# Second PSUM pair, row transfers on SyncE and a new product order in an attention, expert and swish kernel

## The chip, the cores and the metric

The kernel runs on one core of a Trainium2 chip. The metric is device time in microseconds: the median of three runs of the kernel before is 1480.46 us (1477.26 to 1486.97). One execution was profiled: 1479.06 us, its span 1477.0 us, with a mean granted TensorE clock of 0.939 of full speed. All durations below are of that execution.

## The reference

Three layers follow each other, on 4608 tokens of 512 numbers:

```python
scores = scale * (q_c @ k_c.T); attn = softmax(scores); x = attn @ v_c   # chunks of 64
expert_idx = argmax(normalised x @ normalised expert_emb.T / tau)        # one of 8 experts
h = max(x[mask] @ w1[e], 0); x[mask] = gate_w * (h @ w2[e])              # 512 -> 1024 -> 512
h = x @ w_in; g = h * sigmoid(1.702 * h); out = g @ w_out                # 512 -> 2048 -> 512
```

## The kernel before

**Attention** (to about 235 us) makes the tokens x, stores them in DRAM (`xs`) as two 16-bit halves, and sorts them by expert: two tables `mtab` in DRAM hold, at the sorted place of a token, its scale and its number (the sum of the two tables is the entry).

**The expert stage** (about 235 to 750 us) goes over 39 tiles of 128 sorted tokens. For tile i:
- `find(i)` reads the 128 entries of both tables (tile `mt`), by an indirect DMA that POOL issues;
- `fetch(i)` adds the two (POOL) and gathers the tokens (`xg`, an indirect DMA of POOL);
- `turn(i)` transposes them by a DMA of SyncE into `xTm`, of which there are two;
- `mm1(i)` is the first layer: 96 products of 128x128 in two PSUM banks `ph`; ACT (line 895) writes the high half of `hT`, DVE (line 896) the low half;
- `mm2(i)` is the second layer in a bank `py`; `mm2_evac(i)` scales the result on ACT and DVE into the row tile `y` and stores it to `ys` by an indirect DMA of POOL (line 955).

The loop issues, for tile i: `mm1(i)`, `turn(i+2)`, `fetch(i+3)`, `find(i+4)`, `swap(i+1, 1)`, `mm2(i-1)`, `swap(i, 2)`, `mm2_evac(i-1)`, and one step `dec`. `swap` splits the next expert's weights (ACT line 786, DVE line 791) and loads the ones after, under an `If` that is taken only where a tile begins a new expert. The first matmul of `mm1` waits for the bank, the third for the low half of the split of w1, or, where no split is made, for DVE's branch past it (line 840); the splits and the branches stand behind `hT` in DVE's program.

One step of `dec` reads a block of the swish weights (64-bit numbers), rebuilds 32-bit ones on DVE (lines 1222, 1223, 1226, 1229), and makes sums and halves of the previous block: ACT takes the high half (line 1119), POOL subtracts it for the low half (line 1120) and makes differences (line 1128). There are 32 blocks, 16 of `w_in` and 16 of `w_out`; a block of `w_out` sees four such pieces.

**The swish stage** (about 750 to 1477 us) goes over 9 groups j of 512 tokens. `up(j, s)`, four times, makes the hidden values; `down(j)` multiplies by `w_out` with seven products in place of eight, each of 48 matmuls, operands `G[o]`. The hidden values of the four quarters s are `zq[s, ...]`; `mix1` to `mix4` make the sums that four of the products need (`put(o, s, z)`: ACT high half, POOL low half into `G[o]`). `later` is a list of such steps, `mixes(n)` issues n of them, and `more` issues the sums of the next group. A product accumulates on a bank: X takes products 0, 4 and 5, V takes 3 and 6. Between two products on one bank, `keep` copies the sum so far to SBUF on ACT (`t1`, `t2`, `t5`). The weights of the products come by a ring of three loads of 1 MB on SyncE's queue.

Each engine runs its own program in the order in which it is written, and every DMA of SyncE waits for the DMA eight before it on that queue.

Of the kernel before, what the change touches and what calls it, by code (L numbers as in the profile page):

```python
# [9 lines left out]
F32 = mybir.dt.float32  # L10
# [7 lines left out]
ENG = mybir.EngineType  # L18
# [16 lines left out]
def kernel(  # L35
# [13 lines left out]
    nc = tc.nc  # L49
    B, H, S, D = q.shape  # L50
    NT, DM = out.shape
    NE = emb.shape[0]
# [10 lines left out]
    SURE = 39  # L63
    NPART = 24
    NSURE = 3
# [8 lines left out]
    ps = ctx.enter_context(tc.tile_pool(name="ps", bufs=1, space=PSUM))  # L74
# [6 lines left out]
    mtab = [dr.tile([NE * NT, 2], F32, name=f"mtab{a}") for a in range(2)]  # L81
    YP = 2 * DM + 8
    ys = dr.tile([NT + 128, YP], F16, name="ys")
# [59 lines left out]
    for t in vt:  # L143
# [15 lines left out]
        out=tri16, in_=ones16, pattern=[[1, 128]], compare_op=ALU.is_gt, fill=0.0,  # L159
# [19 lines left out]
    for m_, op_ in ((lt_m, ALU.is_lt), (le_m, ALU.is_le)):  # L179
        nc.vector.tensor_tensor(  # L180
            out=m_, in0=io_e.unsqueeze(1).to_broadcast([128, NE, NE]),
# [9 lines left out]
    for t in mtab:  # L191
        nc.sync.dma_start(
            out=t.rearrange("(p a r) c -> p a (r c)", p=128, a=4),
            in_=ztab.to_broadcast([128, 4, NE * NT * 2 // 512]),
# [396 lines left out]
    idx_g = const.tile([128, MAXT], I32, name="idx_g")  # L591
    idx_y = const.tile([128, MAXT], I32, name="idx_y")
# [168 lines left out]
    def reg(ap, engines, hi):  # L761
        return nc.values_load(ap, engines=engines, min_val=0, max_val=hi)
# [83 lines left out]
    mt_t, xg_t, xTm_t, hT_t = {}, {}, {}, {}  # L846

    def find(i):
        mt_t[i] = [mo.tile([128, 2], F32, tag=f"mt{a}", name=f"mt{a}", bufs=6) for a in range(2)]
        for a in range(2):  # L850
            nc.gpsimd.indirect_dma_start(  # L851
                out=mt_t[i][a][:, :], out_offset=None, in_=mtab[a][:, :],
                in_offset=bass.IndirectOffsetOnAxis(ap=idx_g[:, i:i + 1], axis=0),
            )
# [20 lines left out]
    ph_t = {}  # L875

    def mm1_part(i, q):

        xT = xTm_t[i]
        if q == 0:  # L880
            ph_t[i] = [ps.tile([128, 4, 128], F32, tag="A", name="ph", bufs=2) for _ in range(2)]
            hT_t[i] = mo.tile([128, 2 * KF, 128], F16, tag="hT", name="hT", bufs=2)
        p, hT = ph_t[i][q // 2], hT_t[i]
        for f in (2 * q, 2 * q + 1):
            fs = slice(f * 128, (f + 1) * 128)
            for c in range(KD):
                for wt, a in ((w1H, c), (w1H, KD + c), (w1L, c)):
                    nc.tensor.matmul(  # L888
                        p[:, f % 4], wt[:, c, fs], xT[:, a, :],
                        start=(c == 0 and a == 0 and wt is w1H), stop=(c == KD - 1 and wt is w1L),  # L890
                    )
        if q % 2 == 0:
            return
        hi, lo = (hT[:, o + q // 2 * 4:o + q // 2 * 4 + 4] for o in (0, KF))
        nc.scalar.activation(out=hi, in_=p, func=AF.Relu)  # L895
        nc.vector.scalar_tensor_tensor(out=lo, in0=p, scalar=0.0, in1=hi, op0=ALU.max, op1=ALU.subtract)  # L896
        if q == 3:
            xTm_t.pop(i)
            ph_t.pop(i)
# [23 lines left out]
    def mm2_evac(i):  # L923
        hT_t.pop(i)
        p = py_t.pop(i)
        mt = mt_t.pop(i)
        y = mo.tile([128, YP], F16, tag="y", name="y", bufs=2)
        ysq = mo.tile([128, DM], F16, tag="ysq", name="ysq", bufs=1)
        s = mo.tile([128, 4], F32, tag="ys", name="ysc", bufs=2)
        si = s.bitcast(I32)  # L930
        c_i = mt.bitcast(I32)[:, 0:1]
        tail = y[:, 2 * DM:YP].bitcast(I32).rearrange("p (a two) -> p a two", two=2)
        n = (YP - 2 * DM) // 4
        nc.scalar.activation(out=ysq, in_=p, func=AF.Square, scale=2.0 ** -20, accum_out=s[:, 0:1])  # L934
        nc.vector.tensor_scalar(si[:, 3:4], c_i, EXP_BITS, None, op0=ALU.bitwise_and)
        nc.vector.tensor_copy(tail[:, :, 0], mt.bitcast(I32)[:, 1:2].to_broadcast([128, n]))
        nc.vector.tensor_scalar(s[:, 0:1], s[:, 0:1], Y_MIN * 2.0 ** -40, None, op0=ALU.max)
        nc.vector.tensor_scalar(
            si[:, 1:2], si[:, 0:1], 24, 23, op0=ALU.logical_shift_right, op1=ALU.logical_shift_left
        )  # L940
        nc.vector.tensor_scalar(
            si[:, 1:2], si[:, 1:2], -1.0, float((BIAS + Y_TOP - 20) << 23), op0=ALU.mult, op1=ALU.add
        )
        nc.vector.scalar_tensor_tensor(  # L944
            out=si[:, 2:3], in0=c_i, scalar=MAN_BITS, in1=si[:, 1:2], op0=ALU.bitwise_and, op1=ALU.bitwise_or
        )
        nc.scalar.activation(out=y[:, 0:DM], in_=p, func=AF.Copy, scale=s[:, 2:3])  # L947
        nc.vector.scalar_tensor_tensor(
            out=y[:, DM:2 * DM], in0=p, scalar=s[:, 2:3], in1=y[:, 0:DM], op0=ALU.mult, op1=ALU.subtract
        )  # L950
        nc.vector.scalar_tensor_tensor(
            out=tail[:, :, 1], in0=si[:, 3:4].to_broadcast([128, n]), scalar=float(BIAS << 23),
            in1=si[:, 1:2].to_broadcast([128, n]), op0=ALU.add, op1=ALU.subtract,
        )
        nc.gpsimd.indirect_dma_start(  # L955
            out=ys[:, :], out_offset=bass.IndirectOffsetOnAxis(ap=idx_y[:, i:i + 1], axis=0),
            in_=y[:, :], in_offset=None,
        )


    def v_due(n):
# [288 lines left out]
    dec = big_split()  # L1250
    yT_t, id_t, R_t = {}, {}, {}
    NRING = 3
    PROD = ((B11, 0), (B21, 1), (T4, 2), (T1, 3), (T2, 4), (T3, 5), (B22, 6))
    LASTD = NSURE + 33
    for i in range(NSURE, SURE):
        mm1(i)
# [69 lines left out]
    banks = [ps.tile([128, 512], F32, tag="A", name="pa", bufs=2) for _ in range(2)]  # L1326
    banks.append(ps.tile([128, 512], F32, tag="C", name="pc"))
    banks += [ps_d.tile([128, 512], F32, tag="B", name="pb", bufs=2) for _ in range(2)]
    banks += [ps_d.tile([128, 512], F32, name=f"pd{a}") for a in range(2)]
    banks.append(gb)  # L1330
    nb = [0]

# [13 lines left out]
    def two(t):  # L1346
        return t.rearrange("p (a t) -> p a t", a=2)

    def add(o, x, p, op=ALU.add):
        nc.vector.tensor_tensor(out=o, in0=x, in1=p, op=op)  # L1350

    def keep(o, p):
        nc.scalar.activation(out=o, in_=p, func=AF.Copy)  # L1353
# [67 lines left out]
    zq = {}  # L1421
# [27 lines left out]
    def put(o, s, z):  # L1449
        parts(z, *(G[o][:, a, 2 * s:2 * s + 2, :] for a in range(2)))  # L1450

    def mix1(s):
        add(zq[s, 2], zq[s, 7], zq[s, 2])
        put(3, s, zq[s, 2])

    def mix2(s):
        add(zq[s, 7], zq[s, 0], zq[s, 7], ALU.subtract)
        add(zq[s, 0], zq[s, 2], zq[s, 0], ALU.subtract)
        put(4, s, zq[s, 0])

    def mix3(s):
        put(5, s, zq[s, 7])
# [5 lines left out]
    def mixes(n):  # L1468
        while n > 0 and later:
            f, s = later.popleft()  # L1470
            f(s)
            n -= 1
# [92 lines left out]

    def down(j):

        for s in range(1, 4):
            later.append((mix1, s))
        for f in (mix2, mix3, mix4):  # L1570
            for s in range(1, 4):
                later.append((f, s))
        nxt_j = j + 1 < NG
        more = sums(j + 1) if nxt_j else iter(())

        def prod(n, p, first):
            w, o = ring.pop((j, n)), PROD[n][1]
            product(
                p, lambda a, c, tt: G[o][:, a, c, tt * 128:(tt + 1) * 128],
                lambda b, c: w[:, b, c * 256:(c + 1) * 256], KG // 2, first,  # L1580
            )
            jn, m = (j, n + NRING) if n + NRING < 7 else (j + 1, n + NRING - 7)
            if jn < NG:
                load_w(jn, m)

        def new(h):
            o_t[j, h] = mem("hT", F32, 1024).rearrange("p (t d) -> p t d", t=2)
            return [o_t[j, h][:, :, d * 256:(d + 1) * 256] for d in range(2)]

        X, W, Y, V = bank(), bank(), bank(), bank()  # L1590
        flush()
        prod(0, X, True)
        mixes(2)
        keep(t1, X)
        mixes(1)
        if nxt_j:
            scales_a(j + 1)
        prod(1, W, True)
        o11, o12 = new(0)
        add(o11, two(t1), two(W))  # L1600
        mixes(3)
        prod(2, Y, True)
        mixes(6)
        prod(3, V, True)
        keep(t5, V)
        if nxt_j:
            scales_b(j + 1)
        for _ in range(3):
            next(more, None)
        prod(4, X, False)  # L1610
        keep(t2, X)
        for _ in range(3):
            next(more, None)
        prod(5, X, False)
        o21, o22 = new(1)
        add(o22, two(t5), two(X))
        keep(c22, X)
        add(o21, two(c22), two(Y))
        scaled(j, 1)
        store(j, 1, 0)  # L1620
        prod(6, V, False)
        add(o12, two(t2), two(V))
        store(j, 1, 1)
# [53 lines left out]
```

## Time and profile before

| | |
|---|---|
| runs | 1480.46 us median (1477.26 to 1486.97) |
| profiled execution | 1479.06 us, span 1477.0 us |
| TensorE (PE) busy | 1280.8 us, 87% of the span |
| VectorE (DVE) busy | 1071.5 us, 73% |
| GpSimd (POOL) busy | 866.6 us, 59% |
| ScalarE (ACT) busy | 727.3 us, 49% |

The busy shares are means over three stages with different limits, so a change in a stage is read from that stage: which engine PE waits for there, and what that engine waited for.

### The profile page before, as it was taken

The page shows a single profiled execution, that of the slowest core. Times are in us where ns is not written, and L with a number is a line of the kernel's source. Part 1 is how long each engine was busy: PE and PEld are TensorE (multiplying, and loading weights), DVE is VectorE, ACT ScalarE, POOL GpSimd, SP SyncE. Part 2 cuts the span into 40 slices and gives each one's busy share as a digit, 9 for nine tenths or more (in the row PEclk, how much of TensorE's full clock was granted, in tenths as well). Part 3 has the DMA queues.
Part 4 walks back from the last instruction along what each step waited for, and adds up shares of the span by engine and source line. Part 5 has one row for each costly group of instructions (what it writes and reads, how often), then busy time and mean ns, then how long its engine had stood idle before and what let it go on. Part 6 is the DMA issues. An engine that isn't in the chain of part 4 may idle for free. (4 is left out here: it accounts for less than half of the span.)

```text
span 1477.0 us, 35208 instructions
## 1 busy us (share of the span) xinstructions
PE 1280.8 (87%) x14098; PEld 1054.7 (71%) x14098; DVE 1071.5 (73%) x1888; ACT 727.3 (49%) x1285; POOL 866.6 (59%) x787
## 2 busy tenths in 40 slices
PE   6766755778899898899869999999999999989996
PEld 5655545556666675666648888888888888878885
DVE  4878886636675769987448687877969696958682
ACT  7976753224443434553435363636464545545452
POOL 1445556545666666676227576666767575746564
PEclk9998866899999999999979999999999999999998
DMA  9988845275774657777522526251626262533412
GB/s 206 243 151 185 178 98 151 63 220 149 187 217 115 198 137 229 239 218 196 127 85 60 184 45 212 31 193 51 183 75 172 87 161 98 143 115 92 167 42 102
DMA packets 220662, 214.32 MB, mean 145 GB/s; under 512 B 131000, under 2 KB 176056, under 8 KB 220480
## 3 DMA queue, kind: packets, MB, share of 16 engines
q1 hardware_dynamic: 200320, 174.46, 45.4%
q0 software_dynamic: 12768, 30.10, 6.0%
q10 hardware_dynamic: 7392, 7.36, 1.5%
q8 instruction: 112, 1.84, 0.6%
q14 instruction: 70, 0.57, 0.1%
HBM read 155.06 MB, written 37.14 MB: 130 GB/s over the span
## 5 line engine op out<-in xcount | busy, mean ns | idle before, releaser
L1415 PEld LDWEIGHTS <-wS 128*128 128x128 f16 x3024 | 297.7, 98 | 52.6 <-issue 16.5
L888 PE MATMUL ph<-xTm,w1HL 128*128 128x128 f16 x3744 | 241.6, 230 | 55.6 <-DVE hT L896 19.4
L888 PEld LDWEIGHTS <-w1HL 128*128 128x128 f16 x3744 | 232.6, 104 | 73.0 <-issue 28.8
L921 PE MATMUL py<-w2HL,hT 128*128 128x512 f16 x936 | 209.0, 380 | 0.0
L921 PEld LDWEIGHTS <-hT 128*128 128x128 f16 x936 | 90.3, 98 | 102.0 <-issue 1.1
L955 POOL DMA_INDIRECT ys<-y,idx_y x39 | 38.8, 996 | 135.8 <-ACT sg L1119 45.8
L851 POOL DMA_INDIRECT mt<-mtab,idx_g x78 | 88.2, 1130 | 32.9 <-issue 18.9
L1350 DVE TENSOR_TENSOR zA<-zA 128x512 f32<-128x512 f32 x72 | 92.6, 1286 | 13.0 <-POOL w2HL L1357 12.4
L1561 POOL DMA_INDIRECT out_dram<-hT,idc x36 | 35.4, 984 | 106.7 <-DMA out_dram<-hT,idc 43.2
L1415 PEld LDWEIGHTS <-w2HL 128*128 128x128 f16 x864 | 84.6, 98 | 9.8
L1415 PEld LDWEIGHTS <-w1HL 128*128 128x128 f16 x864 | 84.5, 98 | 9.8
L896 DVE SCALAR_TENSOR_TENSOR hT<-ph,hT 128x512 f16<-128x512 f32 x78 | 50.8, 682 | 49.3 <-ACT hT L895 48.5
L417 POOL TENSOR_TENSOR x<-x,sx_all 128x512 f32<-128x512 f32 x33 | 34.4, 1042 | 74.3 <-ACT P L351 29.1
L1439 ACT ACTIVATE zA<-zA 128x512 f32<-128x512 f32 x72 | 45.1, 629 | 59.5 <-DVE zA L1436 34.0
L1415 PEld LDWEIGHTS <-stgB 128*128 128x128 f16 x432 | 46.9, 109 | 31.5 <-issue 21.6
L895 ACT ACTIVATE hT<-ph 128x512 f16<-128x512 f32 x78 | 43.5, 589 | 49.1 <-PE ph L888 47.1
L494 POOL DMA_INDIRECT mtab<-meta,pi_all x36 | 37.2, 1032 | 48.0 <-DMA mtab<-meta,pi_all 24.7
L1357 POOL TENSOR_TENSOR w1HL<-zA,w1HL 128x512 f16<-128x512 f32 x36 | 49.6, 1377 | 26.7 <-ACT w1HL L1353 26.4
L934 ACT ACTIVATE ysq<-py 128x512 f16<-128x512 f32 x39 | 23.1, 593 | 84.0 <-PE py L921 76.2
L947 ACT ACTIVATE y<-py,ysc 128x512 f16<-128x512 f32 x39 | 26.8, 688 | 75.7 <-DVE ysc L944 75.7
L1229 DVE SCALAR_TENSOR_TENSOR fo<-raw_o,d_t 128x512 int32<-128x512 int32 x16 | 61.5, 3841 | 1.0
L1415 PE MATMUL pb<-stg,wS 128*128 128x256 f16 x456 | 56.1, 276 | 5.7 <-ACT stg L1353 3.7
(372 smaller groups left out, 3249.2 us busy)
## 6 DMA issues: line engine op xcount, KB each, us to landing
ring<-wod SPq DMA_DIRECT2D x63, 1024.0 KB
stg<-in_moe_w_dram SPq DMA_DIRECT2D x14, 1024.0 KB
stgB<-in_moe_w_dram SPq DMA_DIRECT2D x14, 1024.0 KB
vt<-in_v_dram SPq DMA_DIRECT2D x64, 144.0 KB
xs<-xr SPq DMA_DIRECT2D x36, 256.0 KB
raw_o<-in_moe_w_in_dram SPq DMA_DIRECT2D x16, 512.0 KB
raw_o<-in_moe_w_out_dram SPq DMA_DIRECT2D x16, 512.0 KB
wod<-sg ACTq DMA_DIRECT2D x4, 1792.0 KB
```

The lines of the kernel that those rows point to most:

```text
L494: nc.gpsimd.indirect_dma_start(out=mtab[t % 2][:, :], out_offset=bass.IndirectOffsetOnAxis(ap=pi_all[:, t:t + 1], axis=0), in_=meta[:, t, ...
L851: nc.gpsimd.indirect_dma_start(out=mt_t[i][a][:, :], out_offset=None, in_=mtab[a][:, :], in_offset=bass.IndirectOffsetOnAxis(ap=idx_g[:, i ...
L888: nc.tensor.matmul(p[:, f % 4], wt[:, c, fs], xT[:, a, :], start=(c == 0 and a == 0 and wt is w1H), stop=(c == KD - 1 and wt is w1L),)
L895: nc.scalar.activation(out=hi, in_=p, func=AF.Relu)
L896: nc.vector.scalar_tensor_tensor(out=lo, in0=p, scalar=0.0, in1=hi, op0=ALU.max, op1=ALU.subtract)
L921: nc.tensor.matmul(p, hT[:, a, :], wt[:, c, :], start=st, stop=sp)
L955: nc.gpsimd.indirect_dma_start(out=ys[:, :], out_offset=bass.IndirectOffsetOnAxis(ap=idx_y[:, i:i + 1], axis=0), in_=y[:, :], in_offset=None,)
L1229: nc.vector.scalar_tensor_tensor(out=fi, in0=hi, scalar=-(1 << 31), in1=t, op0=ALU.bitwise_and, op1=ALU.bitwise_or)
L1350: nc.vector.tensor_tensor(out=o, in0=x, in1=p, op=op)
L1357: eng.tensor_tensor(out=lo, in0=x, in1=hi, op=ALU.subtract)
L1415: nc.tensor.matmul(dst, lhs(a, k, ab), rhs(b, k), start=first and ab == 0 and k == 0 and m == 0, stop=(k == n - 1 and m == 2), skip_group_ ...
L1439: nc.scalar.activation(out=z, in_=z, func=AF.Sigmoid, scale=1.702 * 2.0 ** -G_EXP)
```

## The change

Three edits. The PSUM banks of the first expert layer: tiles from number 3 on with an odd number take two banks of a second pair ("D", the ones that the swish stage used under other names), the even ones the first pair ("A"). The rows of the table and of the result: for tiles 3 to 38 the entries are read, and for all 39 the result rows are stored, by plain DMAs of SyncE, whose row comes from a register that SyncE loads from `idx_g` or `idx_y`. The products of `down`: the one on T2 comes before the one on T1, the steps `mix1` and `mix2` are cut differently, and `t2` and `t5` are kept in the other order.

```diff
     def find(i):
+        row = reg(idx_g[0:1, i:i + 1], [ENG.SP], NE * NT - 128) if NSURE <= i < SURE else None
         for a in range(2):
+            if row is not None:
+                nc.sync.dma_start(out=mt_t[i][a][:, :], in_=mtab[a][bass.ds(row, 128), :])
+                continue
             nc.gpsimd.indirect_dma_start(
...
-            ph_t[i] = [ps.tile([128, 4, 128], F32, tag="A", name="ph", bufs=2) for _ in range(2)]
+            pool, tag = (ps_d, "D") if i >= NSURE and i % 2 else (ps, "A")
+            ph_t[i] = [pool.tile([128, 4, 128], F32, tag=tag, name="ph", bufs=2) for _ in range(2)]
...
-        nc.gpsimd.indirect_dma_start(
-            out=ys[:, :], out_offset=bass.IndirectOffsetOnAxis(ap=idx_y[:, i:i + 1], axis=0),
-            in_=y[:, :], in_offset=None,
-        )
+        if i < NSURE:
+            nc.sync.dma_start(out=ys[i * 128:(i + 1) * 128, :], in_=y)
+        elif i < SURE:
+            row = reg(idx_y[0:1, i:i + 1], [ENG.SP], NT)
+            nc.sync.dma_start(out=ys[bass.ds(row, 128), :], in_=y)
+        else:
+            nc.gpsimd.indirect_dma_start(
...
-    PROD = ((B11, 0), (B21, 1), (T4, 2), (T1, 3), (T2, 4), (T3, 5), (B22, 6))
+    PROD = ((B11, 0), (B21, 1), (T4, 2), (T2, 4), (T1, 3), (T3, 5), (B22, 6))
...
-    banks += [ps_d.tile([128, 512], F32, name=f"pd{a}") for a in range(2)]
+    banks += [ps_d.tile([128, 512], F32, tag="D", name="pd", bufs=2) for _ in range(2)]
...
     def mix1(s):
         add(zq[s, 2], zq[s, 7], zq[s, 2])
-        put(3, s, zq[s, 2])
-
-    def mix2(s):
         add(zq[s, 7], zq[s, 0], zq[s, 7], ALU.subtract)
         add(zq[s, 0], zq[s, 2], zq[s, 0], ALU.subtract)
         put(4, s, zq[s, 0])
+
+    def mix2(s):
+        put(3, s, zq[s, 2])
...
+        mixes(6)
+        prod(2, Y, True)
         mixes(3)
-        prod(2, Y, True)
-        mixes(6)
-        prod(3, V, True)
-        keep(t5, V)
+        prod(3, X, False)
+        keep(t2, X)
...
-        prod(4, X, False)
-        keep(t2, X)
+        prod(4, V, True)
+        keep(t5, V)
...
         prod(5, X, False)
```

What moves on POOL in the expert stage, in an ordinary tile with a block of `w_out` (`mt` are table entries, `xg` the gathered tokens, `d_f`, `fo` and `sg` are blocks of the swish weights). Before:

```order
L858 TENSOR_TENSOR mt_9848<-mt_9848,mt_9849 128x2
L864 DMA xg<-xs,mt_9848 128x1024
L851 DMA mt_10066<-mtab_76,idx_g 128x2
L851 DMA mt_10067<-mtab_77,idx_g 128x2
L840 UNCONDITIONAL_BRANCH
L830 UNCONDITIONAL_BRANCH
...
L955 DMA ys<-y,idx_y 4736x1032
L1128 TENSOR_TENSOR d_f<-fo 128x512
L1120 TENSOR_TENSOR sg<-fo,sg 128x256
```

The changed kernel, the same place:

```order
L862 TENSOR_TENSOR mt_10338<-mt_10338,mt_10339 128x2
L868 DMA xg<-xs,mt_10338 128x1024
L1139 TENSOR_TENSOR d_f<-fo 128x512
L840 UNCONDITIONAL_BRANCH
L830 UNCONDITIONAL_BRANCH
...
L1131 TENSOR_TENSOR sg<-fo,sg 128x256
```

The two table reads and the store of y are gone from POOL; the difference `d_f<-fo` now follows the gather at once.

On SyncE in a tile with a block of `w_in`, behind the conditional loads of weights. Before:

```order
L830 UNCONDITIONAL_BRANCH x2
L1108 DMA raw_o_4585<-in_moe_w_in_dram 128x1024
L872 DMA_TRANSPOSE xTm<-xg 128x8x128
L762 TENSOR_LOAD nf_i
L762 ISA x2
```

The changed kernel:

```order
L830 UNCONDITIONAL_BRANCH x2
L762 TENSOR_LOAD idx_y
L762 ISA x2
L964 ISA
L964 DMA ys<-y 128x1032
L1119 DMA raw_o_4604<-in_moe_w_in_dram 128x1024
L876 DMA_TRANSPOSE xTm<-xg 128x8x128
L840 UNCONDITIONAL_BRANCH
L762 TENSOR_LOAD idx_g
...
L853 DMA mt_7465<-mtab_76 128x2
...
L853 DMA mt_7466<-mtab_77 128x2
```

In the changed kernel the store of y stands ahead of the block load and the transpose, the table reads behind the transpose.

On ACT in `down`, from the last high half of the mixes to the last copy (`stgB_4578<-` and `stgB_4598<-` are the copies t5 and t2, `stg_81` the sums of the next group, `R` its scales). Before:

```order
L1353 ACTIVATE op_13278<-zA 128x512
L1353 ACTIVATE stgB_4578<-pb 128x512
L1353 ACTIVATE R<-pb 128x512
L1353 ACTIVATE stg_81<-xTm 128x512
L1353 ACTIVATE stgB_4578<-pa 128x512
L1353 ACTIVATE stg_81<-xg 128x512
```

The changed kernel:

```order
L1364 ACTIVATE op_13998<-zA 128x512
L1364 ACTIVATE stgB_4598<-pa 128x512
L1364 ACTIVATE R<-pb 128x512
L1364 ACTIVATE stg_81<-xTm 128x512
L1364 ACTIVATE stgB_4598<-pb 128x512
L1364 ACTIVATE stg_81<-xg 128x512
```

The copy that stands behind the first high half of the next group's sums was that of X (bank pa); it is now that of V (bank pb).

## Rows read from the trace of the kernel before

**Rows 1.** Windows, the expert stage's steady part and the swish stage; columns named.

```profile
core 0: us, PE busy (x) PEld busy (x) DVE busy (x) ACT busy (x) POOL busy (x), PEclk, DMA share, GB/s
343.06:745.90 402.84, 361.24 (x3865) 260.86 (x3863) 295.10 (x500) 179.00 (x305) 241.96 (x246) 0.96 0.66 188
758.00:1464.00 706.00, 676.51 (x6044) 597.13 (x6042) 532.45 (x654) 354.20 (x618) 449.48 (x348) 0.98 0.38 114
```

**Rows 2.** PE's products on the ring's weights: idle time before (us, times), by releaser.

```profile
  ACT stgB L1353: 20.1, 9
```

**Rows 3.** Timeline, one `down`: start, us, engine, line, operation, [idle before <-releaser].

```profile
958.51 1.57 DVE L1350 TENSOR_TENSOR zB<-zB 128x512 f32<-128x512 f32 x1
...
976.47 5.40 PE L1415 MATMUL pa<-ring,stg 128*128 128x256 f16 x48
...
983.12 0.63 ACT L1353 ACTIVATE stg<-xTm 128x512 f16<-128x512 f32 x1 [5.52 <-DVE xTm L1350]
...
983.66 0.58 ACT L1353 ACTIVATE stgB<-pa 128x512 f32<-128x512 f32 x1
...
984.29 7.07 PE L1415 MATMUL pa<-ring,stgB 128*128 128x256 f16 x48 [2.42 <-ACT stgB L1353]
```

**Rows 4.** Windows, the product after that wait (columns as in rows 1).

```profile
984.29:991.36 7.07, 7.07 (x50) 5.70 (x50) 3.71 (x4) 1.78 (x3) 3.68 (x3) 0.76 0.28 114
```

**Rows 5.** Line 1350, the additions on `zA`: duration ns min/median/max, first and last start.

```profile
L1350 DVE TENSOR_TENSOR zA<-zA x72: 679/1636/1659, 776.4 to 1444.9; 128x512 f32<-128x512 f32 x72
```

**Rows 6.** Waits of PE, 290 to 750 us: us in total, times, longest us.

```profile
PE ph L888 <- DVE hT L896: 19.4, 10, 3.8
PE ph L888 <- ACT w1HL L786: 8.6, 3, 3.5
...
PE ph L888 <- DVE w1HL L791: 7.6, 11, 1.5
```

**Rows 7.** Timeline, an ordinary tile of the expert stage, columns as in rows 3.

```profile
582.48 0.93 ACT L1119 ACTIVATE sg<-fo 128x256 f16<-128x256 f32 x2
...
582.79 0.42 DVE L1222 TENSOR_SCALAR d_t<-d_t 128x512 f32<-128x512 f32 x1
...
583.68 1.00 POOL L955 DMA_INDIRECT ys<-y,idx_y  x1 [5.72 <-ACT sg L1119]
583.71 0.70 DVE L1226 SCALAR_TENSOR_TENSOR d_t<-raw_o,d_t 128x512 int32<-128x512 int32 x1
584.51 4.43 DVE L1229 SCALAR_TENSOR_TENSOR fo<-raw_o,d_t 128x512 int32<-128x512 int32 x1
584.71 1.27 POOL L1128 TENSOR_TENSOR d_f<-fo 128x512 f32<-128x512 f32 x1
...
587.24 1.14 POOL L1120 TENSOR_TENSOR sg<-fo,sg 128x512 f16<-128x512 f32 x1
...
589.59 0.36 PE L888 MATMUL ph<-xTm,w1HL 128*128 128x128 f16 x2 [3.51 <-DVE hT L896]
590.25 6.74 PE L888 MATMUL ph<-xTm,w1HL 128*128 128x128 f16 x94 [0.29 <-DVEq L840]
```

**Rows 8.** Line 1229, blocks of w_out, columns as in rows 5.

```profile
L1229 DVE SCALAR_TENSOR_TENSOR fo<-raw_o,d_t x16: 692/3780/4509, 514.4 to 695.0; 128x512 int32<-128x512 int32 x16
```

**Rows 9.** Line 791, the splits of w1, columns as in rows 5.

```profile
L791 DVE SCALAR_TENSOR_TENSOR w1HL<-stg,w1HL x32: 654/1213/1226, 208.0 to 718.9; 128x1024 f16<-128x1024 f32 x28, 128x512 f16<-128x512 f32 x4
```

**Rows 10.** Page, costliest groups: the stores of y (busy, mean ns, idle before).

```profile
L955 POOL DMA_INDIRECT ys<-y,idx_y x39 | 38.8, 996 | 135.8 <-ACT sg L1119 45.8
```

**Rows 11.** Timeline, PE at the stage's start.

```profile
309.92 7.04 PE L888 MATMUL ph<-xTm,w1HL 128*128 128x128 f16 x96 [8.26 <-DMA xTm<-xg]
```

**Rows 12.** Timeline, between expert and swish stage.

```profile
733.00 2.75 SPq L1296 DMA_DIRECT2D ring<-wod  x3
...
744.38 0.17 DVE L936 COPY y<-mt 128x2 int32<-128x2 int32 x1 [0.21 <-DMA ys<-y,idx_y]
...
755.13 1.29 DVE L1350 TENSOR_TENSOR xg<-yT 128x512 f32<-128x512 f16 x2 [3.41 <-DMA mt<-mtab,idx_g]
```

More of the change, by code (lines that the diff above doesn't have):

```diff
@@ L954, in mm2_evac @@
         )
-        nc.gpsimd.indirect_dma_start(
-            out=ys[:, :], out_offset=bass.IndirectOffsetOnAxis(ap=idx_y[:, i:i + 1], axis=0),
-            in_=y[:, :], in_offset=None,
-        )
+        if i < NSURE:
[5 more added lines that the diff above has]
+            nc.gpsimd.indirect_dma_start(
+                out=ys[:, :], out_offset=bass.IndirectOffsetOnAxis(ap=idx_y[:, i:i + 1], axis=0),
+                in_=y[:, :], in_offset=None,
+            )
     def v_due(n):
@@ L1566, in down @@
     def down(j):
-        for s in range(1, 4):
-            later.append((mix1, s))
-        for f in (mix2, mix3, mix4):
+        for f in (mix1, mix2, mix3, mix4):
             for s in range(1, 4):
```

## The prediction

> **What bounds the kernel now.** I read the windows first, then PE's waits stage by stage, then the timeline around the largest wait of each. In the windows [rows 1] the reader is to see that PE is busy 676.5 of 706 us in the swish stage, but 361.2 of 402.8 in the steady expert stage: nobody has more to do than PE, and what can be won is its waits and what the clock costs after them. In the swish stage the products on the ring's weights waited 20.1 us, nine times, all for ACT's copy of a sum [rows 2]: once in each group. In the expert stage PE's waits go by DVE (the low half of hT) and by the split of w1 [rows 6]. The timeline [rows 7] shows why DVE is late: its last step on a block of swish weights took 4.43 us, against 0.69 at its fastest [rows 8], and it ended when POOL's run of four operations did.
>
> **The order of the products.** Before, product 4 accumulates on X, the copy t2 of X follows, and product 5 writes X again. The copy cannot begin before product 4 ends, and stands on ACT behind a high half that waited 5.52 us for DVE [rows 3]; PE stood still for 2.42 us. In the new order T2 on X, then T1 on V, then T3 on X: between two products on one bank lies another, 5.40 us long at full clock [rows 3]. The wait leaves: 20.1 us in nine groups, eight near the 2.42 of the row and one of 0.75.
>
> After the wait the product took 7.07 us instead of 5.40 [rows 3], at a granted clock of 0.76 [rows 4], so part of it ran at 1.2 GHz instead of 2.4; before the wait PE had run products back to back. Six of the nine products after a wait look like this (6.86 to 7.07, the other three 5.40), together 9.7 us over. Without the wait I take them to run as the others. Term A: -20.1 - 9.7 = **-29.8 us**.
>
> What is late next? The copy of V now stands behind the same high half on ACT. In the old trace that place was reached at 984.24; product 6, which writes V, would begin at 976.47 + 2 x 5.40 = 987.3. Margin 3.0 us. The other deadline is G[4], now wanted by the fourth product instead of the fifth. It needs three additions a quarter instead of one, nine for three quarters, from 958.51 on [rows 3]; at 0.68 to 1.66 us each [rows 5] they end between 964.6 and 973.4, and ACT and POOL take 0.6 and about 1.6 us more. The fourth product would begin at 976.47 - 5.40 = 971.1 and asks for the last quarter three quarters of its way in, at 975.1. At the slow end this is 0.5 us late, at the likely middle 3 early. Twelve additions remain twelve, so DVE's later work keeps its times. Bounds of A: 0, if the wait reappears elsewhere in full, and -29.8.
>
> **The rows on SyncE.** POOL loses 36 x 2 table reads and all 39 stores of y. The stores cost it 38.8 us busy, and 135.8 us of standing idle before them [rows 10], because the store waits for y while work that needs no y stands behind it. In the tile shown [rows 7] POOL waited 5.72 us, stored until 584.68, and only then ran its four operations, to 588.38; DVE's line 1229 ended at 588.94 and PE began 3.51 us late. Without the store the first of the four (1.27 us) needs nothing that is late and runs ahead; the other three, 2.4 us, need ACT's high halves, of which the first is done near 582.95. They end near 585.4, DVE then does lines 1226 and 1229 in 1.4 us, by 586.8 instead of 588.9: 2.1 us earlier. In a tile whose second pair of pieces is done it is less, and where the first piece needs ACT about the 1.0 us of the store. The bounds are 0 and 2.1 us; I take 1.2 a tile, nearer to the row than to nothing.
>
> The Trainium skill (SBUF — State Buffer, section "Who interferes with whom") says that DVE and POOL share a pair of ports under an exclusive lock, held for one instruction by whoever starts first. The trace differs: line 1229 started 0.2 us before POOL's operation [rows 7] and still waited out the whole run. The Trainium skill's page also lets one-input operations in a two-port mode take the pair; by it lines 1222 and 1223 (0.42 us each) would be held up too once POOL starts earlier, 1.25 us would be left of the 2.1 and some 0.7 of the 1.2, and the sum would be 6 us worse.
>
> 1.2 us off each of the ten waits for hT (four of them are shorter, 3.4 us together) takes 3.4 + 7.2 = 10.6 of their 19.4 us; the waits for the split of w1, 16.2 us at six changes of expert, lose 6 x 1.2 = 7 [rows 6]. Against it, the operation that runs ahead now falls on DVE's split of w1, which was never disturbed (1213 ns median, 1226 at most [rows 9]): 0.7 to 1.3 us in about half of the eight changes, +4. The granted clock of 0.96 over 361 us [rows 1] is some 14 us of lost speed after such waits (the product run behind the 3.51 us wait took 6.74 us [rows 7]); with a third of the waiting gone I take 4 back. Term B: -10.6 - 7 + 4 - 4 = -17.6.
>
> SyncE's own queue gains two register loads, two reads and a store per tile. They stand between a transpose and the block load, which waits for line 1229 anyway, later than y is ready; and a transpose is wanted two tiles, some 20 us, after its issue. I cost that at nothing. Its cover is gone only where the queue carries megabytes:
> - At the stage's start 4 MB of weights hold up the transpose for which PE waited 8.26 us [rows 11]. The reads of tiles 4 and 5 now pass through the same queue: 0 to +4, I take +2.
> - At the end the store of tile 36 now lies behind three ring loads, 3.1 MB issued from 733.00 on [rows 12]. At the stage's 188 GB/s [rows 1] these end near 750; tile 38's first copy into the same buffer stood at 744.38 and waited 0.21 us for that store. So it may come 5 us later, in part under the wait for the last mm2; and the 3.41 us that DVE waited for a transfer at 755.13 may go or stay. -3 to +5, I take +2.
>
> The Trainium skill's page DMA: Bandwidth & Descriptors ("Queues, rings and completion order") says the same against this edit: within one row a DMA engine takes descriptors in ring order, while it goes round between rows packet by packet; a store on POOL's row would pass the ring loads. By it the +2 would be the +5.
>
> **The second PSUM pair.** It removes the first matmul's wait for the bank. But the third matmul waits for DVE's branch, which stands behind the same low half (0.29 us later, after the first two had run [rows 7]). So PE gets two matmuls, 0.27 us, ahead in ten places; less than 3 us, I take -1. This edit does not do what it says.
>
> **Sum**, against the profiled 1479.06: -29.8 - 17.6 - 1 + 4 = -44.4, or 1434.7. The median of the runs lies 1.4 above that execution: **1436 us**.
>
> **Rivals.**
> - *Only the products pay.* POOL's earlier run simply holds DVE earlier, or DVE's other work takes the time. For it: DVE serves ACT's y and hT in fixed order. Against: 3 us of each line 1229 are waiting [rows 8]. 1480.5 - 29.8 + 4 = 1455.
> - *The wait in down moves* to product 6 or to the fourth product. It decides when DVE's additions come 3.0 us later than now; from 5.4 us on all is given back: 1480.5 - 14.6 = 1466.
> - *DVE was the bound of the expert stage.* Then what it gains adds up from tile to tile after each change of expert, and most of the 36 us of [rows 6] and the clock's 14 go: B near -40, 1415.
> - *Slower: POOL's run falls on the splits.* If not one operation but the whole run of 3.7 us holds each of the 16 sets of splits (8 changes, w1 and w2), 59 us come on top and B's gain goes: 1480.5 - 29.8 + 4 + 59 = 1514. It turns the sign from 1.6 us a set on. Against: three of the four operations need ACT, which splits first.
>
> **How the numbers follow.** Forecast 0.52, only the products 0.18, DVE the bound 0.15, the wait moves 0.10, slower 0.05. The range 1412 to 1464 takes the forecast with its bounds, the first rival, and over half of the third. One per cent, about what can be told from no change, is 1465.7 to 1495.3: the rival at 1466 falls on both sides. Faster 0.90, within 1% 0.06, slower 0.04.
>
> **What would show it.** Right: no wait on ACT between the products of down, all of them 5.40 us; line 1229 near 2 us instead of 3.8; waits for hT halved; PE still waiting for DVE's branch at the third matmul. Wrong: a wait of product 6 on the copy of V, splits above 1.3 us, PE waiting for a transpose, the table reads landing after POOL asks for them.

## The result, and the profile after

The changed kernel took 1439.37 us (median of 4 runs, 1435.42 to 1442.98), against 1483.72 us of the kernel before beside it: a ratio of 0.970 (95% interval 0.965 to 0.975). The forecast was 1436. The profiled execution has a span of 1441.2 us, 35.8 less than before. A sum that comes out is no proof of its terms, so the span is cut at two marks: the first matmul of `mm1`, and the matmul on `onesB` that opens the swish stage.

| us | attention | expert | swish | sum |
|---|---|---|---|---|
| before | 235.2 | 515.4 | 726.4 | 1477.0 |
| after | 240.5 | 481.2 | 719.5 | 1441.2 |
| difference | +5.3 | -34.1 | -6.9 | -35.8 |
| forecast | 0 | -17.6 - 1 + 4 | -29.8 | -44.4 |

The attention stage was not changed; over the 14 profiled executions of this study it lasts 226.5 to 240.5 us. The expert stage gave more than twice its forecast, the swish stage less than a quarter. One execution tells a stage to some microseconds only: e4 below, whose swish stage is the same code, spent 713.5 us in it. The windows of the two stages, of the kernel before (columns as in [rows 1]):

```profile
235.22:750.57 515.35, 444.40 (x4769) 324.28 (x4766) 359.48 (x694) 207.46 (x360) 297.70 (x306) 0.94 0.63 176
750.57:1477.00 726.43, 680.36 (x6057) 599.10 (x6057) 537.08 (x661) 356.76 (x622) 453.09 (x352) 0.97 0.37 113
```

and of the changed kernel:

```profile
240.48:721.71 481.23, 431.37 (x4769) 314.28 (x4766) 330.47 (x693) 206.37 (x360) 191.52 (x194) 0.96 0.71 189
721.71:1441.20 719.49, 674.31 (x6057) 596.15 (x6057) 533.29 (x661) 352.21 (x622) 452.46 (x351) 0.98 0.38 114
```

Read the first two numbers of each line against each other. In the swish stage PE stands idle 726.43 - 680.36 = 46.1 us before and 45.2 after: the waits of the old order are gone, and as many have come. What is left of the gain, 6.1 us, is the same 6057 matmuls running faster. In the expert stage the same 4769 matmuls take 13.0 us less, PE's idle time falls by 21.1 us, and DVE is busy 29.0 us less with the same work.

**The expert stage.** PE's waits from 290 us to the stage's end, of the changed kernel, against [rows 6] (us in total, times, longest us):

```profile
PE ph L893 <- DMA xTm<-xg: 13.3, 3, 7.4
PE ph L893 <- DVEq L840: 8.5, 7, 2.2
PE ph L893 <- DVE w1HL L791: 6.1, 8, 1.3
PE ph L893 <- ACTq L840: 4.2, 3, 1.8
PE ph L893 <- ACT w1HL L786: 3.3, 2, 1.7
```

The waits for hT are gone by name; with the second PSUM pair the same wait is now booked on the branch (line 840). Before, the branch had two more rows of its own:

```profile
PE ph L888 <- DVEq L840: 4.1, 12, 0.4
...
PE ph L888 <- ACTq L840: 1.8, 1, 1.8
```

So hT and branch together fell from 19.4 + 4.1 + 1.8 = 25.3 to 12.7 us, the splits from 16.2 to 9.4. The waits for the transpose did not grow to 13.3 us: 5.59 of them stand at 290.27, and the kernel before has the same wait at 289.43, just outside the window of [rows 6]. New is one of 0.28 us. DVE's four steps on a block are lines 1233, 1234, 1237 and 1240 now (1222, 1223, 1226 and 1229 before), line 791 splits the weights (columns as in [rows 5]):

```profile
L1233 DVE TENSOR_SCALAR d_t<-d_t x32: 415/419/428, 313.6 to 671.5; 128x512 f32<-128x512 f32 x32
L1234 DVE TENSOR_SCALAR d_t<-d_t x32: 426/1372/1395, 314.1 to 672.0; 128x512 int32<-128x512 int32 x32
L1237 DVE SCALAR_TENSOR_TENSOR d_t<-raw_o,d_t x32: 691/1098/1651, 314.6 to 673.3; 128x512 int32<-128x512 int32 x32
L1240 DVE SCALAR_TENSOR_TENSOR fo<-raw_o,d_t x16: 691/692/1526, 506.8 to 674.0; 128x512 int32<-128x512 int32 x16
L791 DVE SCALAR_TENSOR_TENSOR w1HL<-stg,w1HL x32: 682/1216/2297, 207.8 to 692.4; 128x1024 f16<-128x1024 f32 x28, 128x512 f16<-128x512 f32 x4
```

The last step now takes its shortest time, 0.69 us, where [rows 8] had 3.78. Holding has not ended: it falls on the second and third step, 1.37 and 1.10 us where the old trace had 0.43 and 0.70. Over the stage the four steps keep DVE busy for 115.0 us instead of 148.5; at their shortest times they would take some 71. An ordinary tile of the changed kernel, to be laid beside [rows 7]:

```profile
588.54 1.27 POOL L1139 TENSOR_TENSOR d_f<-fo 128x512 f32<-128x512 f32 x1
...
592.14 0.78 POOL L1131 TENSOR_TENSOR sg<-fo,sg 128x256 f16<-128x256 f32 x1 [2.32 <-ACT sg L1130]
592.42 0.78 DVE L1234 TENSOR_SCALAR d_t<-d_t 128x512 int32<-128x512 int32 x1
592.88 0.91 POOL L1139 TENSOR_TENSOR d_f<-fo,d_f 128x256 f32<-128x256 f32 x1
593.23 1.10 DVE L1237 SCALAR_TENSOR_TENSOR d_t<-raw_o,d_t 128x512 int32<-128x512 int32 x1
593.74 1.60 POOL L1131 TENSOR_TENSOR sg<-fo,sg 128x512 f16<-128x512 f32 x1
594.43 1.46 DVE L1240 SCALAR_TENSOR_TENSOR fo<-raw_o,d_t 128x512 int32<-128x512 int32 x1
595.82 1.27 DVE L901 SCALAR_TENSOR_TENSOR hT<-ph,hT 128x512 f16<-128x512 f32 x2
```

POOL's first operation now runs early, at 588.54, and POOL then waits 2.32 us for ACT. The other three follow each other without a gap, and DVE's steps go in turns with them: each is held by about one operation of POOL and not by the run (the last one took 1.46 us in this tile). POOL is held as well, 0.78 and 0.91 us for the operations that took 0.67 and 0.72 before:

```profile
585.93 0.67 POOL L1120 TENSOR_TENSOR sg<-fo,sg 128x256 f16<-128x256 f32 x1
586.56 0.72 POOL L1128 TENSOR_TENSOR d_f<-fo,d_f 128x256 f32<-128x256 f32 x1
```

DVE's last step ends at 595.89, POOL's last operation at 595.34, and hT follows. Why DVE waited out the whole run in the old tile and takes turns in this one is not shown by these rows.

**The swish stage.** A `down` of the changed kernel (columns as in [rows 3]):

```profile
944.52 5.40 PE L1426 MATMUL pb<-ring,w2HL 128*128 128x256 f16 x48
...
949.64 0.63 ACT L1364 ACTIVATE stg<-xTm 128x512 f16<-128x512 f32 x1 [3.99 <-DVE xTm L1361]
...
949.76 5.40 PE L1426 MATMUL pa<-ring,stgB 128*128 128x256 f16 x48
950.18 0.58 ACT L1364 ACTIVATE stgB<-pb 128x512 f32<-128x512 f32 x1
```

The wait of [rows 3] is gone and the product on T3 takes 5.40 us, not 7.07; so in all nine groups. The copy of V ends at 950.76, 4.2 us before product 6 begins at 955.00. But PE's waits of the stage now have rows that stood there once before (2.7 us):

```profile
PE pa L1426 <- DVE stgB L1361: 7.2, 2, 4.0
PE pd L1426 <- DVE stgB L1361: 5.4, 3, 2.0
...
PE pb L1426 <- DVE stgB L1361: 4.0, 2, 2.3
...
PE pc L1426 <- DVE stgB L1361: 2.3, 1, 2.3
...
PE gb L1426 <- DVE stgB L1361: 1.4, 1, 1.4
```

Nine waits, 20.3 us: again one in each group, in the second quarter of `up`. The chain of waits through the longest of them, in order of time (start, us, what):

```profile
962.58 3.74 DMA out_dram<-hT,idc
...
967.09 5.13 DMA out_dram<-hT,idc
...
973.00 1.01 POOL out_dram L1572
...
975.15 1.16 POOL w2HL L1368
...
976.33 1.65 DVE zA L1361
...
978.00 0.70 DVE zA L1361
...
978.73 0.69 DVE zA L1361
979.42 0.62 DVE pc L1361
...
980.67 0.69 DVE stgB L1361
...
981.40 1.47 PE pa L1426 x12
```

Read it from below. PE wanted bank pa, which DVE empties with `stgB<-stgB,pa`; ahead of that on DVE stand three additions on `zA`, the step `mix1` of quarter 0; these write sums that POOL must have read for a low half; and POOL came to that low half only after a store of output rows, which had waited for the store before it. The same place in the kernel before has one addition, and no wait of PE:

```profile
1010.07 0.69 DVE L1350 TENSOR_TENSOR zA<-zA 128x512 f32<-128x512 f32 x1 [1.06 <-POOL w2HL L1357]
...
1011.04 0.70 DVE L1350 TENSOR_TENSOR pc<-stgB,pc 128x512 f32<-128x512 f32 x1 [0.28 <-PE pc L1415]
...
1013.46 1.47 PE L1415 MATMUL pa<-yT,wS 128*128 128x256 f16 x12
```

### The profile page after: what moved, and what is told of

The parts are those of the page before. It is cut to its first block, busy times and chain, and to the rows that moved or that the text cites. A ratio compares the mean times of both kernels' runs of the same rounds, so it can differ in the third digit from the quotient of the medians.

```text
span 1441.2 us, 35556 instructions
## 1 busy us (share of the span) xinstructions
PE 1263.9 (88%) x14098; PEld 1043.1 (72%) x14098; DVE 1034.0 (72%) x1888; ACT 721.1 (50%) x1285; POOL 759.7 (53%) x676
## 5 line engine op out<-in xcount | busy, mean ns | idle before, releaser
L893 PE MATMUL ph<-xTm,w1HL 128*128 128x128 f16 x3744 | 230.1, 225 | 35.5 <-DMA xTm<-xg 13.3
L893 PEld LDWEIGHTS <-w1HL 128*128 128x128 f16 x3744 | 222.6, 101 | 50.8 <-issue 14.9
L1426 PEld LDWEIGHTS <-w2HL 128*128 128x128 f16 x864 | 84.5, 98 | 10.6
L1426 PEld LDWEIGHTS <-w1HL 128*128 128x128 f16 x864 | 84.6, 98 | 9.8
L1131 POOL TENSOR_TENSOR wS<-d_f,wS 128x512 f16<-128x512 f32 x28 | 35.9, 1283 | 95.0 <-ACT wS L1130 95.0
L1361 DVE TENSOR_TENSOR zA<-zA 128x512 f32<-128x512 f32 x72 | 73.5, 1021 | 16.4 <-POOL w2HL L1368 15.1
L341 DVE TENSOR_REDUCE mx<-sp 128x8 f32<-128x512 f32 x36 | 24.8, 689 | 51.2 <-PE sp L334 51.0
L312 ACT ACTIVATE kuT<-tp 64x512 f32<-64x512 f32 x72 | 45.2, 628 | 16.4 <-PE tp L307 15.4
L1426 PE MATMUL pa<-stg,wS 128*128 128x256 f16 x432 | 51.6, 273 | 1.9 <-ACT stgB L1364 1.9
```

The lines of the kernel that those rows point to most:

```text
L312: lambda r=r, p=p, dst=dst: nc.scalar.activation(out=dst[:, :, r], in_=p[r * 64:(r + 1) * 64], func=AF.Copy)
L893: nc.tensor.matmul(p[:, f % 4], wt[:, c, fs], xT[:, a, :], start=(c == 0 and a == 0 and wt is w1H), stop=(c == KD - 1 and wt is w1L),)
L1131: nc.gpsimd.tensor_tensor(out=L_, in0=f, in1=H_, op=ALU.subtract)
L1426: nc.tensor.matmul(dst, lhs(a, k, ab), rhs(b, k), start=first and ab == 0 and k == 0 and m == 0, stop=(k == n - 1 and m == 2), skip_group_ ...
```

## The experiments

Twelve kernels, each timed beside the kernel before on the same chip; that one took 1477.8 us beside e1 to e4, 1478.3 beside e5 to e8 and 1474.6 beside e9 to e12, and gains in us are of these. Stage lengths are of the profiled execution of each.

| kernel | ratio (95%) | expert us | swish us |
|---|---|---|---|
| e1, order of products alone | 0.992 (0.989 to 0.995) | 511.6 | 723.4 |
| e2, both row transfers alone | 0.979 (0.975 to 0.984) | 486.4 | 727.8 |
| e3, PSUM pairs alone | 1.000 (0.998 to 1.003) | 511.3 | 732.8 |
| e4, all but the pairs | 0.968 (0.964 to 0.973) | 483.8 | 713.5 |
| e5, all, quarter 0 cut as before | 0.954 (0.950 to 0.958) | 483.3 | 694.3 |
| e6, all, a store of out later | 0.966 (0.960 to 0.971) | 483.2 | 708.9 |
| e7, e5 and e6 | 0.953 (0.950 to 0.957) | 483.7 | 693.3 |
| e8, store of y later on POOL, alone | 0.980 (0.975 to 0.985) | 487.7 | 732.3 |
| e9, stores of y on SyncE alone | 0.983 (0.979 to 0.986) | 484.2 | 730.3 |
| e10, table reads on SyncE alone | 0.994 (0.993 to 0.996) | 510.2 | 728.9 |
| e11, order, quarter 0 as before, alone | 0.978 (0.974 to 0.983) | 513.7 | 697.9 |
| e12, e8 and e11 | 0.963 (0.959 to 0.967) | 489.7 | 699.9 |

### The three edits apart

**e1**: the kernel before with the diff's `PROD`, `mix1`, `mix2`, `later` and `down`, and nothing else of it.

> The kernel before with the new order of the products and the new cut of the mixes alone. The theory read from the two traces (the wait in down leaves, but the three additions and the stores of out hold DVE in the next group's up, and PE waits 1.4 to 4.0 us there once a group): the swish stage goes from 726.4 to about 719.5 us, so about -7 us, 1476. The theory of the prediction (term A whole): -29.8 us, 1453; then the new waits in up would have to come from the other two edits.

1465.4 us, ratio 0.992: some 12 us gained (7 to 16). The swish stage lasts 723.4 us; in the six executions with the old order it lasted 726.4 to 732.8. Nine waits of PE for DVE in the second quarter of `up`, 21.0 us, stand there with neither SyncE's rows nor the pairs in the kernel: the loss belongs to the new order's own cut. The forecast of 29.8 falls.

**e2**: `find` and `mm2_evac` of the change, alone.

> The kernel before with the table reads and the stores of y on SyncE alone. Theory from the two traces: the expert stage loses about 34 us (515.4 to 481.4), the swish stage keeps its 726 and the nine waits for the copy of X: 1449. Theory of the prediction: -17.6 + 4, about -14: 1469. If the second PSUM pair is needed for the rest, it lies between and the kernel without the pairs shows the same loss.

1447.4 us, 31 us gained (24 to 38), all in the expert stage (486.4); the swish stage keeps the nine waits for the copy of X. The expert term is twice the forecast, without the pairs.

**e3**: the `ph` tiles and the two banks `pd` of the change, alone.

> The kernel before with the second PSUM pair alone. Prediction: less than 3 us, -1; the third matmul still waits for DVE's branch, and waits of 0.29 us behind the first two matmuls become the whole wait. Rival: the pair frees PE of hT, the ten waits of 19.4 us go to half or less, -10 us and more.

No change. The waits of this kernel, against the 25.3 us of hT and branch before:

```profile
PE ph L889 <- DVEq L840: 16.1, 11, 4.1
PE ph L889 <- ACTq L840: 8.7, 5, 3.6
```

24.8 us: the wait for hT has changed its name and kept its length. This is what the prediction meant by an edit that does not do what it says.

**e4**: the changed kernel with the old line for `ph`.

> The changed kernel without the second PSUM pair (rows and products stay). Prediction: the pair is worth 1 us, so 1440 (+1). Rival: with POOL's run out of DVE's way the pair carries a large part of what the expert stage gained: +10 us and more, and waits for hT instead of for the branch.

0.968, against 0.970 with the pairs: no difference that these intervals tell. With POOL's run out of the way the pairs carry nothing that can be measured either.

### Where the gain of the products went

**e5**:

```diff
     def mix1(s):
         add(zq[s, 2], zq[s, 7], zq[s, 2])
-        add(zq[s, 7], zq[s, 0], zq[s, 7], ALU.subtract)
-        add(zq[s, 0], zq[s, 2], zq[s, 0], ALU.subtract)
-        put(4, s, zq[s, 0])
+        if s == 0:
+            put(3, s, zq[s, 2])
+        else:
+            two_sums(s)      # the three lines removed above
     def mix2(s):
-        put(3, s, zq[s, 2])
+        if s == 0:
+            two_sums(s)
+        else:
+            put(3, s, zq[s, 2])
```

> The changed kernel, but the mixes of quarter 0, which run in up, are cut as before (one addition in the first step, two in the second); quarters 1 to 3 keep the new cut. Theory 1 (the two more additions ahead of the sums that empty PE's banks cost the eight waits in up, 18.9 us): some 2.0 us leave each, some 16 us together, about 3 of waiting left where a store of out is late, 0.96 of the time before. Theory 2 (POOL's store of out, for which the low half and so the additions wait, makes the waits): they stay above 10 us, and at most 6 us are gained.

1410.3 us, 0.954. No wait for DVE is left in `up`, and the window of the stage reads:

```profile
714.70:1409.00 694.30, 668.98 (x6057) 594.25 (x6057) 526.09 (x661) 354.22 (x622) 454.69 (x351) 0.98 0.38 118
```

PE idles 25.3 us, not 45.2, and is busy 5.3 us less. The two additions are what it takes: without them no wait comes, though the stores stand where they stood.

**e6**: in `up`, `if s == 1: more()` becomes `if s == 2: more()`, and the second store of `tail` goes with it.

> The changed kernel, but the last store of the previous group's rows goes out in up of quarter 2 instead of quarter 1, so POOL makes the low halves without waiting for the store before. Theory 1: one us off the six ordinary waits, 2 to 3 off the two long ones (3.96 and 3.27), some 11 of 18.9 us, 7 to 8 left. Theory 2: nearly all 18.9 leave.

0.966 (0.960 to 0.971), which overlaps the changed kernel's interval. Both numbers expected were wrong: of the eight waits of 18.9 us, 12.8 us remain, not 7 to 8 and not none (with the first group's wait, 14.2 of 20.3). The long ones became short, all nine now lie between 1.41 and 1.82 us:

```profile
973.89 1.47 PE L1426 MATMUL pa<-yT,wS 128*128 128x256 f16 x12 [1.41 <-DVE stgB L1361]
...
1049.56 1.47 PE L1426 MATMUL pa<-yT,wS 128*128 128x256 f16 x12 [1.41 <-DVE stgB L1361]
```

So the store made the long waits (3.96 and 3.27 us), and about 1.4 to 1.8 us in every group come from the additions alone: two more of 0.69 us each are 1.38.

**e7**: both edits.

> Both of these at once on the changed kernel. Theory 1 and 2 agree: no wait in up for DVE is left, the swish stage near 700 us (term A of the prediction whole), about 0.955 of the time before. If the stage stays above 710, a third cause holds it.

0.953 and 693.3 us in the stage: the same as e5. Once the two additions are gone, the store's place adds nothing that can be measured.

**e11**: e1 with the diff of e5.

> The kernel before with the order of the products and the new cut for quarters 1 to 3 alone; quarter 0 is cut as before. Theory: term A of the prediction whole, -29.8 us: the nine waits and most of the slow products leave and nothing comes in up, the swish stage near 696 us, 0.979 of the time before. Rival: part of it was owed to the other edits, 0.985 and more.

0.978: 32 us gained (25 to 39), the stage 697.9 us, and PE waits once for DVE in `up`, 2.8 us, as the kernel before did. Term A is there in full when quarter 0 keeps its cut.

### What the rows gained

**e8**: nothing goes to SyncE; POOL's store of y is issued behind the step on the swish weights.

```diff
-        mm2_evac(i - 1)
-        if i < LASTD:
-            next(dec, None)
-        if i == LASTD:
-            next(dec, None)
+        rows = mm2_evac(i - 1, True)      # returns its indirect store
+        if i <= LASTD:
+            next(dec, None)
+        rows()
+        if i == LASTD:
```

> The kernel before, with POOL's store of y issued behind the step on the swish weights instead of ahead of it; nothing goes to SyncE. Theory 1 (what the rows gained is POOL's order: its operations no longer stand behind a wait for y, so line 1229 is not held): line 1229 near 0.7 us, some 20 to 29 us gained, 1450 to 1458. Theory 2 (it needs the reads and stores gone from POOL): under 10 us gained, line 1229 still 2 us and more.

0.980, as e2. The last step on a block is line 1235 here, the second 1229:

```profile
L1235 DVE SCALAR_TENSOR_TENSOR fo<-raw_o,d_t x16: 691/693/1527, 496.6 to 666.2; 128x512 int32<-128x512 int32 x16
```

```profile
L1229 DVE TENSOR_SCALAR d_t<-d_t x32: 426/1313/1385, 300.6 to 664.2; 128x512 int32<-128x512 int32 x32
```

The same picture as in the changed kernel, with POOL busier than before (316.6 us in the stage, 297.7 before): the four steps take 121.4 us instead of 148.5, and PE waits 14.4 us for hT and branch instead of 25.3. What made DVE's steps so long is the order on POOL, not its load: a store that waits for y stood ahead of work that could run.

**e9** and **e10**: of the diff's `mm2_evac` and `find`, one each.

> The kernel before with the stores of y on SyncE; the table reads stay on POOL. If the wait for y ahead of POOL's run is all there is to the rows edit, this gives as much as the whole edit: the expert stage near 486 us, 0.979 of the time before. If the reads matter too, it gives clearly less (0.985 and more).

> The kernel before with the table reads on SyncE; the stores of y stay on POOL. By the first theory POOL's run still stands behind the wait for y, line 1229 keeps its 2 to 4 us and the ten waits for hT stay: no change, 0.995 to 1.00. By the second it gives what the stores alone do not.

The stores alone give 0.983 (0.979 to 0.986) and an expert stage of 484.2 us: nearly all, and the interval reaches to both of the ratios expected. The reads alone give 0.994 (0.993 to 0.996), some 8 us, where 0 to 7 was expected; the last step on a block (line 1233 in e10) still takes 3.78 us:

```profile
L1233 DVE SCALAR_TENSOR_TENSOR fo<-raw_o,d_t x16: 691/3778/4505, 506.4 to 686.6; 128x512 int32<-128x512 int32 x16
```

Its expert stage, 510.2 us, is hardly below those of the other four executions with POOL's old order (511.3 to 515.4), but PE stands idle 62.6 us in it against 68.6 to 71.0. So part of these 8 us are waits in this stage; what took them away stays open.

**e12**: e11 and e8 together, everything on POOL.

> The same, and the store of y issued on POOL behind the step on the swish weights: neither SyncE rows nor a second PSUM pair. If the two gains add up and need neither: 0.954 to 0.958 of the time before, as the changed kernel with quarter 0 cut as before (0.954). If the reads and stores on POOL cost the path more than these traces show: 0.965 and more.

0.963 (0.959 to 0.967): between the two. The product of the two gains, 0.978 x 0.980 = 0.958, is known to about 0.007, so whether they add up in full can't be told; e5, with its rows on SyncE, is faster by 0.9%. The expert stage of e12 is 6.5 us longer than e5's and its swish stage 5.6. In the latter one wait of 4.67 us for DVE stands, at 1275.87, in the place where the kernel before has its one of 2.7, and e5 has none: POOL came late to the low half there. The rest was not taken apart; the swish stage of the changed kernel and that of e4, the same code, differ by 6.0 us. e5 also has the PSUM pairs, which earned nothing in e3 and e4; so some 13 us are left for SyncE's rows beyond the order on POOL, with their cause open.

## Why the prediction was right, and where it was not

The sum was right: 1436 forecast, 1439.4 measured, inside the range, and faster by over 1%. The two terms that make it were not: their errors lay in opposite directions, 23 us too much in the swish stage and nearly 20 too little in the expert stage. That the total came out is luck.

**Term A, -29.8.** The step that failed is "Twelve additions remain twelve, so DVE's later work keeps its times." The deadlines were worked out for quarters 1 to 3, whose additions stand in `down`. Quarter 0's first step stands in `up`, and the new cut put three additions there instead of one, ahead of the sums that empty PE's banks: 20.3 us of waiting in nine places, where 20.1 had left. The rival "the wait in down moves" had the kind of it and not the place: it named product 6 and the fourth product, and neither waited (product 6 had 4.2 us to spare where the working gave 3.0). That term A's own working was sound otherwise, e11 shows: 726.4 to 697.9 us, and in e5 20.8 us less idle time and 11.4 us less busy time, against -20.1 and -9.7.

**Term B, -17.6.** The mechanism was right, shown by e8 to e10: the store of y ahead of POOL's run. Waits for hT and branch: -12.6 us against -10.6 - 1. Waits for the splits: -6.8 against -7. Mis-sized were two terms of it. The clock: 4 us were taken back, and PE is busy 13.0 us less with the same matmuls, 9.7 of them from 343 us on. Slow first layers are 6.8 of these: before, eight tiles from 343 us on ran the last 88 or 94 products of their first layer in 6.1 to 7.4 us instead of 5.1 to 5.4, in the changed kernel three. A wait cut from 3 us to 2 could give back its slow product whole, not in proportion: before, 94 products took 6.59 us behind a wait of 2.79 (at 627.46) and 5.42 behind one of 1.91 (at 518.94). And of the +4 for POOL's operation on the split of w1 some 1.7 us came, on DVE: line 791 keeps its median of 1.22 us, but the longest is 2.30, and two of the seven sets from 343 us on took 0.7 and 1.1 us longer than the others. So one of the signs of being wrong, splits above 1.3 us, came, at a small price. The time that line 1229 would keep was wrong as well, "near 2 us": it is 0.69.

The prediction priced a rule of the Trainium skill (SBUF — State Buffer, "Who interferes with whom") that one-input operations of DVE can be held by POOL too. Line 1234 is such an operation and went from 0.43 to 1.37 us in the median. Line 1233, another, stayed at 0.42; in e8 the same operation (line 1228 there) was held once in 32 times, for 3.19 us. So the traces agree. The 6 us that it was to cost did not show, since the last step was then held far less.

Costing SyncE's queue at nothing was right in effect, though another sign of being wrong came: the table reads land after POOL asks for them. From 290 us on POOL waited 46.3 us for them in seven places, 15.0 in five before. PE's one new wait for a transpose is the 0.28 us above.

**The small ones.** The pairs: -1 forecast, nothing measured (e3, e4). The start: PE's wait for the transpose was 7.42 us where [rows 11] has 8.26, so the +2 did not come. At the boundary the +2 did not come either; PE's first two waits there, against 4.40 and 3.72 before (two more, of 0.86 and 2.23, are unchanged):

```profile
721.71 0.61 PE L1387 MATMUL pa<-ysq,onesB 128*128 128x512 bf16 x1 [4.31 <-DVE ysq L1380]
727.11 0.37 PE L1426 MATMUL pb<-stg,wS 128*128 128x256 f16 x1 [1.95 <-ACT stg L1364]
```

The rival of POOL's run falling on all the splits is refuted by line 791. Of the rival of DVE as the bound of the expert stage (near -40) the clock's part came, 13.0 of 14 us; of the waits it took away most of 36 us, and 19.4 went, near the forecast's 17.6 + 1. That gains add up from tile to tile was not shown.

## What to carry to other kernels

A step that is cut differently must be followed to every place that issues it: here `mix1` runs in `up` for quarter 0 and in `down` for the others, and the place that was not looked at gave back two thirds of the gain. On an engine that runs in program order, a store that waits for data should stand behind work that needs none; putting it there was worth as much, alone, as moving it to another queue (0.980 in e8, 0.983 in e9). And a total that fits is checked stage by stage before a term of it is believed.

## What the runs showed of the hardware

- DVE's held time does not go by POOL's load: in e8 POOL was busy 316.6 us in the stage against 297.7, and DVE 340.4 against 359.5. Operations of POOL that stand one behind the other held one step of DVE through the whole run in the old tile (4.43 us) and took turns with DVE's steps in the new one.
- In this program each of POOL's indirect stores of output rows waits until the one before has landed, 3.74 and 5.13 us in the chain above.
- The clock after a wait, in the changed kernel: 94 products took 5.42 us after a wait of 2.10 us at 574.94, with a granted clock of 1.00 (2.4 GHz), and 7.05 after one of 2.19 at 610.12, with 0.76 (in part 1.2 GHz):

```profile
574.94 5.42 PE L893 MATMUL ph<-xTm,w1HL 128*128 128x128 f16 x94 [2.10 <-DVEq L840]
...
610.12 7.05 PE L893 MATMUL ph<-xTm,w1HL 128*128 128x128 f16 x94 [2.19 <-DVEq L840]
```
